# Attention and two MLPs on one core: high parts of probabilities on ScalarE, other costs and priorities in the scheduler

## The chip, the cores and the metric

One core of a Trainium2 chip, one launch. TensorE multiplies, VectorE, ScalarE and GpSimd do the elementwise work, SP (SyncE) issues every DMA of this kernel. The metric is the device time of the launch in microseconds (us); less is better.

## The reference

For 4 batches of 8 heads, 576 positions and head size 64: scores = q k^T / 8, a mask that lets a position see its own block of 64 and all earlier ones, softmax, product with v. The heads are laid side by side to x (2304 x 512). Two MLPs follow:

```
x = attention(q, k, v)                                   # 2304 x 512
h = x @ moe_w_in;  x = (max(h,0) + alpha*min(h,0)) @ moe_w_out     # 512 -> 2048 -> 512
h = x @ moe2_w_in; out = (h * sigmoid(1.702 h)) @ moe2_w_out
```

All inputs of attention are fp32; the four weight matrices and alpha arrive as 64-bit values (weights) and fp32, and the result is fp32.

## The kernel before

**Arithmetic.** A product of fp32 precision is made of three matmuls: each operand is split into a high part (a rounded copy, `hi_part`, ScalarE, L120) and a low part (the difference, `lo_part`, L123, on GpSimd or VectorE). So `gemm1` (L207) is 12 matmuls for one block of 128 hidden units, `g2_half` (L245 to 247) and `g2` (L653) likewise. Weights arrive as 64-bit words and are first narrowed on ScalarE and VectorE (`narrow`, L150 to 156), then split.

**Attention** runs in passes, a pass being a batch and a pair of heads. Queries are cut into five tiles `QT` (64 or 128 rows against 64, 192, 320, 448 or 576 keys); tiles 0 to 2 form one group, 3 and 4 another; a group is worked in two slots. The first batch takes its passes group by group (all four pairs for group one, then for group two), the others both groups in one pass. For a slot: `score` (TensorE, L441); `soft` (the minimum on VectorE, L456, the exponential with its sum on ScalarE, L464); when both slots of a group are through, `norm` (VectorE, L473 and 474) makes the factors. Then for each head `high` (L486) writes the factor times the exponentials as fp16, on GpSimd, one instruction per tile, and `rest` (VectorE, L494) writes the same product less that fp16 value, as a second fp16 part. A DMA transpose (L498, issued by SP) turns both parts, `pv` (L519) multiplies them with V, and `pv_out` (ScalarE L531, VectorE L532) adds up and sends x to DRAM. The exponentials have four buffers (`EB`), two per slot, so the exponentials of the next group wait for the rests of this one; scores have two PSUM buffers.

**MoE, first layer, first half** (hidden blocks 0 to 7) runs in eight blocks of 288 tokens as soon as attention has made them, in between the rest of attention: `gemm1`, `gate` (ScalarE L215, VectorE L216), `gate_split` (L120, L123), `g2_half`. It has two PSUM banks, shared with `warm` (L584), 174 filler matmuls on constants that are planned between the slots of the first batch. One bank belongs to the fillers until the last of them, planned behind the scores of the 14th slot, is through; gemm1 of the second hidden block needs that bank. After attention come the second half of the first layer and the whole second layer in blocks of 384 tokens (L207 and L653 in turn).

**What sets the order.** All work is first listed with a kind and a step. `arrange` then simulates the five engines: among the instructions of an engine whose inputs are there, it issues the one with the lowest place, which is the step plus a tenth of the kind's `ORDER` plus the kind's `SHIFT`. Times for that simulation come from `cost` and from the DMA terms in `arrange` (issue, transfer, landing). The order that results is fixed for each engine; on the chip every engine executes its list strictly in order and waits by semaphores. `HI_ACT` names the tiles whose high part goes to ScalarE; it is empty before.

Of the kernel before, what the change touches and what calls it, by code (L numbers as in the profile page):

```python
# [19 lines left out]
DRAM = bass.MemoryType.DRAM  # L20
# [25 lines left out]
    "split x 2": 8, "load w": 9, "load w 2": 9, "load x": 9, "load k": 9.5, "load q": 9.5, "load v": 9.5, "load alpha": 9.6,  # L46
}
SHIFT = {
    "gate": -44.2, "gate 2": -23, "gemm1": 56.7, "gemm1 2": 12.5, "gemm2": 12.8, "half": 58.9, "half out": -42,
    "high": -6.3, "load alpha": 27.7, "load k": 56.1, "load q": -37.1, "load v": -27.1, "load w": -32.6,  # L50
    "load w 2": -53.5, "load x": -33, "narrow": 56.5, "narrow 2": -25.1, "norm": -46.2, "out": -53.7,
    "prep out": 42.4, "prep t": 41.2, "prep v": 41.6, "pv": -10, "pv out": -41.9, "rest": 40.6, "score": 51.7,
    "setup": -24.2, "soft": 19, "split g": -43.8, "split g 2": 4.8, "split w": 7.8, "split w 2": -28.1,
    "split x": 26.4, "split x 2": 57.1, "warm": 56.9,
}
BIG = 1.0e30

# [2 lines left out]
def kernel(  # L60
# [65 lines left out]
    PTB = 2  # L126
    W = {}
    EB = 4
    HI_ACT = ()
    words = {}  # L130

    def load_w(u):
# [159 lines left out]
    def hl_part(j, x, m, n, h):  # L292
        o = 128 * (QT[j][4] + x * QT[j][3])
        return hl[0 if j < 3 else 1][h][0:m, o + 64 * h:o + 64 * h + n]
# [181 lines left out]
    def high(n, h):  # L476
        for y in (n - 1, n):
            stat, es, tiles = st[y, "e"]
            for a, j, off in tiles:
                q0, m, nk, ch, c0 = QT[j]  # L480
                r = stat[0:m, 2, 2 * a + h:2 * a + h + 1]
                o, e = hl_part(j, 0, m, nk, h), es[h][0:m, off:off + nk]
                if j in HI_ACT:
                    act.activation(out=o, in_=e, func=ACTF.Copy, scale=r)
# [51 lines left out]
    for u, (i, g, s) in enumerate(slots):  # L536
        n = 2 * u
# [12 lines left out]
    for i in range(len(passes)):  # L550
# [8 lines left out]
        for z, what in enumerate(todo):  # L559
            n = n0 + z * (cnt - (i == N0)) // len(todo)  # L560
# [110 lines left out]
    for z, (u, f) in enumerate(seq):  # L671
        n = n2 + z
# [5 lines left out]
    for y, u in enumerate(units):  # L678
        n = start[u]
# [10 lines left out]
    for n, order, z, fn, place in sorted(plan, key=lambda o: o[:3]):  # L690
        places.append((len(nc.cur_bb.bb.instructions), place, order == ORDER["warm"]))
        fn()
    arrange(tc, nc, places)


# [17 lines left out]
def free_size(ap):  # L713
    n = 1
    for _, c in list(ap.ap)[1:]:
        n *= c
    return n


def box(ap):  # L720

    t, size, dims = ap.tensor, BYTES[ap.dtype], list(ap.ap)
    if t.space == PSUM:
        return 0, 128, 0, 1 << 20
    pitch = t.shape[-1] if t.space == DRAM else dims[0][0]
    r0, c0 = divmod(ap.offset, pitch)
    r1 = r0 + 1 + sum((n - 1) * s // pitch for s, n in dims if s >= pitch)
    c1 = c0 + 1 + sum((n - 1) * s for s, n in dims if s < pitch)
    return r0, r1, c0 * size // 64 * 64, -(-c1 * size // 64) * 64


def dma_run(ap):

    n = 1
    for s, c in reversed(list(ap.ap)):
        if s != n:
            break
        n *= c
    return n * BYTES[ap.dtype]


def mode(w):

    rows, cols = list(w.ap)[0][1], free_size(w)
    return tuple(32 if n <= 32 else 64 if n <= 64 else 128 for n in (rows, 128 if BYTES[w.dtype] == 4 else cols))


def takes_port(eng, kind, ins, outs):

    if eng == "Pool":  # L750
        return True
    if eng != "DVE" or not ins or any(a.tensor.space == PSUM for a in ins + outs) or kind == "InstTensorReduce":
        return False
    n = max(free_size(a) for a in outs)
    return sum(free_size(a) == n for a in ins) > 1 or "TensorScalar" in kind or "TensorCopy" in kind


def cost(eng, kind, ins, outs):

    n = max(free_size(a) for a in ins + outs)  # L760
    psum = any(a.tensor.space == PSUM for a in ins)
    if eng == "PE":
        mv, w = ins[:2]
        cols, load = free_size(outs[0]) * (2 if mv.dtype == F32 else 1), free_size(w)
        rows = list(w.ap)[0][1]
        each = 13.3 if mv.dtype == F32R else 2.7
        return cols / 2.4 + each, load / 1.2 + 13.3 if BYTES[w.dtype] == 4 else load / 4.8, cols * rows / 128, mode(w)
    if eng == "Activation":
        return (50 if psum else 93) + n / 1.2 + (187 if len(outs) > 1 else 0),
    full = sum(free_size(a) == n for a in ins)  # L770
    if eng == "Pool":
        return (35 + n / 1.2 if not ins else 244 + n / 1.2 if full < 2 else 148 + 2.1 * n),
    if not ins:
        return (40 if outs[0].tensor.space == PSUM else 7) + n / 1.92,
    if psum and len(ins) < 3 or n < 8 or kind == "InstTensorReduce":
        return 65 + n / 0.96,
    if full < 2:
        return 64 + n / 1.92,
    return (129 if len(ins) > 2 else 68) + n / 0.96,


def arrange(tc, nc, places):
# [4 lines left out]
    for x, i in enumerate(nc.cur_bb.bb.instructions):  # L787
        ins, outs = ([a.bass_ap for a in z if getattr(a, "bass_ap", None) is not None] for z in (i.ins, i.outs))
        if type(i).__name__ in ("BassTilePoolBoundary", "InstRegisterMove") or not outs:
            continue  # L790
        while at + 1 < len(places) and places[at + 1][0] <= x:
            at += 1
        k, need = len(todo), set()
        for rw, ap in [(0, a) for a in ins] + [(1, a) for a in outs]:
            t = ap.tensor
            if t.name.startswith("in_"):
                continue
            tag = getattr(t, "tag", None)
            if tag and t.space != DRAM:
                ring = rings.setdefault(tag, [])  # L800
                if t.name not in users:
                    users[t.name] = set()
                    ring.append((t.tag_meta.bufs, users[t.name]))
                users[t.name].add(k)
            rw = rw or t.space == PSUM
            b = box(ap)
            w, r = writes.setdefault(t.name, []), reads.setdefault(t.name, [])
            for z in w + (r if rw else []):
                if z[4] != k and z[0] < b[1] and b[0] < z[1] and z[2] < b[3] and b[2] < z[3]:
                    need.add(z[4])  # L810
            if rw:
                for l in (w, r):
                    l[:] = [z for z in l if not (b[0] <= z[0] and z[1] <= b[1] and b[2] <= z[2] and z[3] <= b[3])]
            (w if rw else r).append((*b, k))
        eng = i.engine.name
        kind = type(i).__name__
        if eng == "PE":
            if places[at][2] and last_pe is not None:
                need.add(last_pe)
            last_pe = k  # L820
        if kind in ("InstDMACopy", "InstDmaTransposeAnt"):
            a = outs[0]
            size = free_size(a) * list(a.ap)[0][1] * BYTES[a.dtype]
            if kind == "InstDMACopy":

                run = min(dma_run(z) for z in ins + outs)
                t = size / run * (8.3 + 0.0368 * run) / 16
                inside = all(z.tensor.space != DRAM and not z.tensor.name.startswith("in_") for z in ins + outs)
                c = (580 if inside else 400 if run > 512 else 500, 2 * t if inside else t, 1000 if outs[0].tensor.space == DRAM or inside else 1600)
            else:  # L830
                c = (0.0046 * size - 100, size / 32768 * 130, 2400 - 0.0046 * size)
            ports.append(False)
        else:
            c = cost(eng, kind, ins, outs)
            ports.append(takes_port(eng, kind, ins, outs))
        todo.append((i, eng, kind, c, places[at][1]))
        preds.append(need)
# [47 lines left out]
    while coming or any(waiting.values()):  # L885
        while coming and coming[0][0] <= now:
            t, k = heappop(coming)
# [4 lines left out]
        for e in names:  # L892
            while waiting[e] and free[e] <= now:
                k = heappop(waiting[e])[1]
                orders[e].append(todo[k][0])
                _, _, kind, c, _ = todo[k]
                if e == "SP":
                    t = now
                    free[e] = t + c[0] + 70
                    end = ring_end = max(t + c[0] + c[2], ring_end) + c[1]  # L900
                elif e == "PE":

                    slow = seen[int(now / TICK) - 1] < 3060
                    t = now + max(0, c[1] * (1 + slow) - pe_last - (now - pe_end))
                    if c[3] != pe_mode:
                        t, pe_mode = max(t, pe_end + DRAIN), c[3]
                    pe_last = (c[0] - 2.7) * 2 if slow else c[0]
                    end = free[e] = pe_end = t + pe_last
                    while t < end:
                        z = min(end, (int(t / TICK) + 1) * TICK + 0.01)  # L910
                        seen[int(t / TICK)] += c[2] * (z - t) / pe_last
                        t = z
# [41 lines left out]
```

## Time and profile before

| | us |
|---|---|
| median of 3 runs | 1084.31 (1083.62 to 1084.81) |
| the profiled execution | 1087.33, span 1085.5 |
| TensorE busy | 1021.4 (94%) |
| VectorE busy | 604.3 (56%) |
| ScalarE busy | 494.7 (46%) |
| GpSimd busy | 462.4 (43%) |

Busy shares are averages over stages with different limits: attention and the first half of the first layer end near 470 us, and TensorE has little idle time after 190 us. PE is TensorE, PEld its weight load, DVE VectorE, ACT ScalarE, POOL GpSimd, and SPq the queue of SyncE. A releaser ("<-ACT e L464") is what ended a wait.

### The profile page before, as it was taken

How to read it: one execution, taken by the hardware profiler on the slowest of the kernel's cores; microseconds unless marked ns; L12 is line 12 of the kernel's file. 1: busy time of each engine (PE TensorE's matmuls, PEld its weight loads, DVE VectorE, ACT ScalarE, POOL GpSimd, SP SyncE). 2: the span in 40 equal slices, each digit the busy share in tenths (PEclk: the TensorE clock that was granted, in tenths of full speed). 3: DMA queues.
4: the chain of work that ended last, by engine and by line, in shares of the span. 5: the costliest groups of instructions: out<-in, count | busy, mean ns of one | idle time of the engine just before them, and what ended most of it. 6: DMA issues, size and time to landing. Idle time of an engine off the chain costs nothing. (4 is left out here: it accounts for less than half of the span.)

```text
span 1085.5 us, 17180 instructions
## 1 busy us (share of the span) xinstructions
PE 1021.4 (94%) x6454; PEld 934.3 (86%) x6454; DVE 604.3 (56%) x1029; ACT 494.7 (46%) x1164; POOL 462.4 (43%) x494
## 2 busy tenths in 40 slices
PE   7776978999999999999999999999999999999998
PEld 4554867989898899999999999899999999999997
DVE  7888998788888885778883236831111121211110
ACT  5664765666566564565543235433223232322322
POOL 4565864656666574644432233422222222222221
PEclk8888999999999999999999999999999999999999
DMA  7897989788989765544643225401000010000000
GB/s 190 189 209 156 209 188 187 138 176 155 175 154 175 147 124 140 168 141 157 202 144 126 81 65 183 146 8 59 1 30 30 1 59 1 30 30 1 30 1 30
DMA packets 257284, 120.28 MB, mean 111 GB/s; under 512 B 213936, under 2 KB 250800, under 8 KB 257200
## 3 DMA queue, kind: packets, MB, share of 16 engines
q1 hardware_dynamic: 257200, 119.18, 46.1%
q8 instruction: 51, 0.84, 0.3%
q14 instruction: 33, 0.27, 0.1%
HBM read 68.82 MB, written 18.87 MB: 81 GB/s over the span
## 5 line engine op out<-in xcount | busy, mean ns | idle before, releaser
L123 POOL TENSOR_TENSOR gs<-g,gs 128x384 fp32r<-128x384 f32 (+1 forms) x208 | 212.8, 1024 | 452.4 <-ACT gs L120 431.8
L207 PE MATMUL h<-xh,wh 128*128 128x384 f32 (+1 forms) x832 | 272.2, 327 | 6.8 <-ACT xo L251 3.7
L207 PE MATMUL h<-xh,wl 128*128 128x384 f32 (+1 forms) x832 | 270.2, 325 | 0.0
L219 DVE TENSOR_TENSOR g<-g,h 128x384 f32<-128x384 f32 x96 | 53.1, 553 | 291.6 <-ACT g L218 291.6
L653 PE MATMUL acc<-wh,gs 128*128 128x512 f32 x576 | 194.9, 392 | 1.5 <-DVE o L663 1.5
L207 PE MATMUL h<-xl,wh 128*128 128x384 f32 x576 | 193.1, 335 | 0.0
L207 PEld LDWEIGHTS h<-xh,wh 128*128 128x128 f32 x832 | 156.3, 188 | 15.3 <-ACT xo L251 5.2
L207 PEld LDWEIGHTS h<-xh,wl 128*128 128x128 f32 x832 | 156.4, 188 | 0.1
L120 ACT ACTIVATE gs<-g 128x384 fp32r<-128x384 f32 (+1 forms) x208 | 103.3, 498 | 106.7 <-DVE g L219 60.9
L218 ACT ACTIVATE g<-h 128x384 f32<-128x384 f32 x96 | 47.0, 490 | 191.6 <-PE h L207 191.6
L486 POOL TENSOR_SCALAR hl<-e,stat 64x64 f16<-64x64 f32 (+4 forms) x160 | 107.7, 688 | 57.1 <-DVE stat L474 28.0
L653 PEld LDWEIGHTS acc<-wh,gs 128*128 128x128 f32 x576 | 108.1, 188 | 22.4 <-DVE o L663 1.3
L494 DVE SCALAR_TENSOR_TENSOR hl<-e,stat,hl 64x64 f16<-64x64 f32 (+4 forms) x160 | 122.7, 800 | 5.7 <-POOL hl L486 4.7
L653 PE MATMUL acc<-wl,gs 128*128 128x512 f32 x288 | 113.7, 395 | 0.0
L207 PEld LDWEIGHTS h<-xl,wh 128*128 128x128 f32 x576 | 108.1, 188 | 4.1
L519 PE MATMUL pv<-pt,vp 128*128 128x256 f16 (+2 forms) x960 | 88.1, 248 | 14.6 <-DMA pt<-hl 10.5
L464 ACT ACTIVATE e<-sc,stat 64x64 f32<-64x64 f32 (+4 forms) x160 | 82.8, 520 | 34.0 <-DVE hl L494 19.2
L653 PE MATMUL acc<-gs,wh 128*128 128x384 f32 x384 | 98.1, 335 | 0.2 <-DVE o L663 0.2
L216 DVE SCALAR_TENSOR_TENSOR g<-g,nalph,h 128x288 f32<-128x288 f32 (+1 forms) x112 | 61.6, 551 | 58.4 <-ACT g L215 57.4
L519 PEld LDWEIGHTS <-vp 128*128 128x128 bf16 x960 | 64.6, 102 | 27.6 <-DMA pt<-hl 14.9
L123 POOL TENSOR_TENSOR wl<-sq,wh 128x512 fp32r<-128x512 f32 x40 | 59.5, 1488 | 61.7 <-ACT wh L120 61.6
L245 PE MATMUL x<-gs,wh 128*128 128x288 f32 x256 | 75.7, 302 | 2.9 <-ACT wh L120 2.4
(65 smaller groups left out, 1708.4 us busy)
## 6 DMA issues: line engine op xcount, KB each, us to landing
rw<-in_moe_w_in_dram SPq DMA_DIRECT2D x32, 512.0 KB, 4.2
rw<-in_moe_w_out_dram SPq DMA_DIRECT2D x32, 512.0 KB, 3.8
nat_q<-in_q_dram SPq DMA_DIRECT2D x24, 288.0 KB, 4.1
nat_k<-in_k_dram SPq DMA_DIRECT2D x16, 288.0 KB, 3.6
nat_v<-in_v_dram SPq DMA_DIRECT2D x16, 288.0 KB, 4.5
xa<-xo SPq DMA_DIRECT2D x32, 144.0 KB, 2.5
o<-xa SPq DMA_DIRECT2D x24, 192.0 KB, 2.5
xl<-xs SPq DMA_DIRECT2D x6, 768.0 KB, 4.9
```

Source lines behind the costliest of these rows:

```text
L120: act.activation(out=dst, in_=src, func=ACTF.Copy, scale=scale_)
L123: eng.tensor_tensor(out=dst, in0=src, in1=hi.bitcast(F32), op=ALU.subtract)
L207: pe.matmul(ps, st_[:, sl], mv[:, c], start=z == 0, stop=z == 3 * KD - 1)
L216: dve.scalar_tensor_tensor(out=g, in0=g, scalar=nalph[:, f:f + 1], in1=ps, op0=ALU.mult, op1=ALU.add)
L218: act.activation(out=g, in_=ps, func=ACTF.Sigmoid, scale=1.702)
L219: dve.tensor_tensor(out=g, in0=g, in1=ps, op=ALU.mult)
L245: pe.matmul(ps, oh[:, sl], gh, start=f == 0, stop=False)
L464: act.activation(out=eo, in_=v[:, h] if len(heads) > 1 else v, func=ACTF.Exp, scale=-1.0, bias=stat[0:m, 0, a:a + 1], accum_out=stat[0:m, ...
L486: pool.tensor_scalar(out=o, in0=e, scalar1=r, scalar2=1.0, op0=ALU.mult, op1=ALU.mult)
L494: dve.scalar_tensor_tensor(out=hl_part(j, 1, m, nk, h), in0=es[h][0:m, off:off + nk], scalar=stat[0:m, 2, 2 * a + h:2 * a + h + 1], in1=hl ...
L519: pe.matmul(o, l, r, start=z == 0, stop=z == len(ops) - 1)
L653: pe.matmul(ps, a, b_, start=f == f0 and z == 0, stop=f == NF - 1 and z == 2)
```

## The change

The set of tiles in `HI_ACT` goes from none to all five. In `high` the branch for ScalarE is then taken for every tile, so all 160 high parts are activations with the factor as a per-row scale:

```
if j in HI_ACT:
    act.activation(out=o, in_=e, func=ACTF.Copy, scale=r)
else:
    pool.tensor_scalar(out=o, in0=e, scalar1=r, scalar2=1.0, op0=ALU.mult, op1=ALU.mult)
```

In the scheduler's simulation, VectorE's reads of PSUM and reductions of 8 or more columns count 155 ns instead of 65 beside the time per column, and DMA landings count 250 ns (plain) or 600 ns (transposes) later. `SHIFT` gets a new value for nearly every kind.

```diff
--- before.py
+++ after.py
@@ -46,12 +46,12 @@
     "split x 2": 8, "load w": 9, "load w 2": 9, "load x": 9, "load k": 9.5, "load q": 9.5, "load v": 9.5, "load alpha": 9.6,
 }
 SHIFT = {
-    "gate": -44.2, "gate 2": -23, "gemm1": 56.7, "gemm1 2": 12.5, "gemm2": 12.8, "half": 58.9, "half out": -42,
-    "high": -6.3, "load alpha": 27.7, "load k": 56.1, "load q": -37.1, "load v": -27.1, "load w": -32.6,
-    "load w 2": -53.5, "load x": -33, "narrow": 56.5, "narrow 2": -25.1, "norm": -46.2, "out": -53.7,
-    "prep out": 42.4, "prep t": 41.2, "prep v": 41.6, "pv": -10, "pv out": -41.9, "rest": 40.6, "score": 51.7,
-    "setup": -24.2, "soft": 19, "split g": -43.8, "split g 2": 4.8, "split w": 7.8, "split w 2": -28.1,
-    "split x": 26.4, "split x 2": 57.1, "warm": 56.9,
+    "gate": -5.6, "gate 2": 3.5, "gemm1": 58, "gemm1 2": 12.5, "gemm2": 12.5, "half": 55.1, "half out": -40.2,
+    "high": 14.8, "load alpha": 30.8, "load k": 48.3, "load q": -16.4, "load v": -13.4, "load w": 42,
+    "load w 2": -8.5, "load x": 21.6, "narrow": 49, "narrow 2": 21.5, "norm": -15, "out": -55.1,
+    "prep out": 29.6, "prep t": 14.3, "prep v": 33.9, "pv": 8.2, "pv out": -26.5, "rest": 11.7, "score": 53.6,
+    "setup": -59.4, "soft": 5.6, "split g": -25.7, "split g 2": 33.6, "split w": 22.7, "split w 2": 22.6,
+    "split x": 28.2, "split x 2": -47.3, "warm": 59.1,
 }
 BIG = 1.0e30
 
@@ -126,7 +126,7 @@
     PTB = 2
     W = {}
     EB = 4
-    HI_ACT = ()
+    HI_ACT = (0, 1, 2, 3, 4)
     words = {}
 
     def load_w(u):
@@ -773,7 +773,7 @@
     if not ins:
         return (40 if outs[0].tensor.space == PSUM else 7) + n / 1.92,
     if psum and len(ins) < 3 or n < 8 or kind == "InstTensorReduce":
-        return 65 + n / 0.96,
+        return (65 if n < 8 else 155) + n / 0.96,
     if full < 2:
         return 64 + n / 1.92,
     return (129 if len(ins) > 2 else 68) + n / 0.96,
@@ -826,9 +826,9 @@
                 run = min(dma_run(z) for z in ins + outs)
                 t = size / run * (8.3 + 0.0368 * run) / 16
                 inside = all(z.tensor.space != DRAM and not z.tensor.name.startswith("in_") for z in ins + outs)
-                c = (580 if inside else 400 if run > 512 else 500, 2 * t if inside else t, 1000 if outs[0].tensor.space == DRAM or inside else 1600)
+                c = (580 if inside else 400 if run > 512 else 500, 2 * t if inside else t, 1250 if outs[0].tensor.space == DRAM or inside else 1850)
             else:
-                c = (0.0046 * size - 100, size / 32768 * 130, 2400 - 0.0046 * size)
+                c = (0.0046 * size - 100, size / 32768 * 130, 3000 - 0.0046 * size)
             ports.append(False)
         else:
             c = cost(eng, kind, ins, outs)
```

## Rows read from the trace of the kernel before

**Rows 1.** Table by stage: window, length, busy us of PE, PEld, DVE, ACT, POOL.
```profile
0.00:109.00 109.00, 78.39 (x495) 54.01 (x495) 88.90 (x166) 61.09 (x157) 59.94 (x77) 0.86 0.84 186
109.00:190.00 81.00, 66.40 (x524) 58.57 (x523) 73.38 (x134) 50.53 (x137) 52.53 (x57) 0.97 0.95 194
190.00:300.00 110.00, 105.85 (x908) 99.48 (x905) 90.61 (x184) 70.83 (x203) 68.79 (x86) 0.99 0.84 159
300.00:400.00 100.00, 95.45 (x817) 89.40 (x815) 86.43 (x170) 63.00 (x189) 62.35 (x78) 1.00 0.80 153
400.00:450.00 50.00, 48.36 (x385) 46.75 (x383) 31.23 (x47) 24.76 (x60) 26.88 (x26) 1.00 0.57 154
```

**Rows 2.** The chain that ended last, in order of time: start, us, what.
```profile
691.16 2.10 PE h L207 x12
```

**Rows 3.** Fillers (L584) by stage: PE, PEld; timeline of PE near 112 us.
```profile
0.00:109.00 109.00, 39.82 (x169) 17.89 (x169) 0.86 0.84 186
...
111.98 0.98 PE L584 MATMUL warm<-mk_l 128*128 128x384 bf16 x5
112.66 0.43 PE L207 MATMUL h<-xh,wh 128*128 128x288 f32 x1
```

**Rows 4.** Timeline of DVE, norm lines (L473) of the first and eighth group.
```profile
23.01 0.83 DVE L473 TENSOR_SCALAR stat<-stat 128x6 f32<-128x6 f32 x1 [0.28 <-ACT e L464]
...
122.46 0.74 DVE L473 TENSOR_SCALAR stat<-stat 128x4 f32<-128x4 f32 x1
```

**Rows 5.** Groups by shape: rests (L494), a high part (L486); busy, mean ns.
```profile
L494 DVE SCALAR_TENSOR_TENSOR hl<-e,stat,hl 128x576 f16<-128x576 f32 x32 | 35.8, 1118 | 0.2
L494 DVE SCALAR_TENSOR_TENSOR hl<-e,stat,hl 128x448 f16<-128x448 f32 x32 | 33.0, 1030 | 1.6 <-POOL hl L486 1.1
...
L486 POOL TENSOR_SCALAR hl<-e,stat 128x576 f16<-128x576 f32 x32 | 29.7, 928 | 0.0
...
L494 DVE SCALAR_TENSOR_TENSOR hl<-e,stat,hl 128x320 f16<-128x320 f32 x32 | 22.3, 697 | 0.8 <-POOL hl L486 0.7
...
L494 DVE SCALAR_TENSOR_TENSOR hl<-e,stat,hl 64x64 f16<-64x64 f32 x32 | 20.9, 655 | 2.7 <-POOL hl L486 2.7
...
L494 DVE SCALAR_TENSOR_TENSOR hl<-e,stat,hl 128x192 f16<-128x192 f32 x32 | 16.0, 501 | 0.4 <-POOL hl L486 0.2
```

**Rows 6.** Rests (L494, DVE), then high parts (L486, POOL) by stage.
```profile
0.00:109.00 109.00, 23.55 (x32) 0.86 0.84 186
109.00:190.00 81.00, 22.16 (x28) 0.97 0.95 194
...
0.00:109.00 109.00, 19.87 (x32) 0.86 0.84 186
109.00:190.00 81.00, 22.36 (x30) 0.97 0.95 194
```

**Rows 7.** Timeline: a rest under high parts, then rests alone.
```profile
215.10 2.05 POOL L486 TENSOR_SCALAR hl<-e,stat 64x64 f16<-64x64 f32 x5 [2.85 <-DVE stat L474]
...
215.45 0.95 DVE L494 SCALAR_TENSOR_TENSOR hl<-e,stat,hl 64x64 f16<-64x64 f32 x1 [0.45 <-POOL hl L486]
...
68.04 0.26 DVE L494 SCALAR_TENSOR_TENSOR hl<-e,stat,hl 64x64 f16<-64x64 f32 x1
...
369.10 1.42 DVE L494 SCALAR_TENSOR_TENSOR hl<-e,stat,hl 128x448 f16<-128x448 f32 x2
```

**Rows 8.** Groups by line and shape: ScalarE copies from SBUF to SBUF.
```profile
L120 ACT ACTIVATE gs<-g 128x288 fp32r<-128x288 f32 x64 | 28.0, 441 | 14.3 <-DVE g L216 14.0
...
L395 ACT ACTIVATE vp<-nat_v 128x576 bf16<-128x576 f32 x32 | 21.7, 679 | 0.6 <-POOL nat_v L396 0.3
```

**Rows 9.** Minimum over 576 columns (L456); PE waits from 0 to 190 us.
```profile
L456 DVE TENSOR_REDUCE stat<-sc 128x1 f32<-128x576 f32 x32 | 23.9, 748 | 0.4
...
PE pv L519 <- DMA pt<-hl: 8.0, 4, 4.0
PE tp L345 <- DMA nat_k<-in_k_dram: 5.1, 3, 2.6
```

## The prediction

> **What bounds the kernel now.** I read the table by stage first. After 190 us TensorE is the bound: it is busy for 95 to 97% of the stretches from 190 to 450 us [rows 1], and the chain that ended last, read next, is matmuls upon matmuls from 691 us on; the row shown is one of its pieces, a gemm1 of 12 matmuls in 2.10 us [rows 2]. The time that TensorE loses lies ahead of that. From 0 to 109 us it is busy for 78.4 us, but 39.8 of these are fillers, the warm matmuls [rows 1, 3]; so 109 - 38.6 = 70 us are lost there. From 109 to 190 us it idles 14.6 us, from 190 to 450 us another 4.2 + 4.5 + 1.6 = 10.3 us [rows 1]. The work of TensorE is fixed, so the kernel gets shorter by what is saved of these, above all of the 70.
>
> What holds the first stage? The MoE matmuls cannot start in earnest before the last fillers are through: five of them run at 111.98 us, and the row right behind is the first full gemm1 at 112.66 us [rows 3]. The fillers are tied in program order to the scores of the first 14 slots, so that moment is set by the pace of attention. The pace is read from the norm line: 23.01 us for the first group, 122.46 us for the eighth, seven periods of 14.2 us [rows 4]. In the first two stages VectorE is the fullest of the elementwise engines: 88.9 of 109 us (82%), then 73.4 of 81 (91%), against ScalarE's 61.1 and 50.5 and GpSimd's 59.9 and 52.5 [rows 1]. A group's chain also runs through it three times (minimum, norm, rest). I take VectorE as the bound of the early pace.
>
> **The change, part by part. What VectorE gets back.** GpSimd loses 160 high parts, 32 of each of five shapes, 62 of them before 190 us [rows 6]. The rest instruction (L494) reads two tiles and runs beside the next tile's high part. Beside GpSimd it is slow: the 64x64 form took 0.95 us from 215.45, inside a run of five high parts that began at 215.10 and lasted 2.05; alone it took 0.26 us, and the forms of 448 and 576 columns together 1.42 us alone [rows 7]. The straight line through these (0.20 us + 1.0 ns per column) gives 0.39 and 0.52 us at 192 and 320 columns, and a mean of (0.26 + 0.39 + 0.52 + 1.42)/5 = 0.52. The means of the run are 0.655, 0.501, 0.697, 1.030 and 1.118 us [rows 5]. Up to 109 us, 32 rests took 23.6 us where 32 x 0.52 = 16.6 would do: 7.0 us too much. From 109 to 190 us 28 took 22.2 against 14.6: 7.6 too much [rows 6]. Bounds: all of it goes (only high parts were in the way), or only their share of GpSimd's time, 19.9 of 59.9 = one third [rows 1, 6], since the splits of weights, gates and V stay on GpSimd. Rests run next to high parts by construction, so I take two thirds: 4.7 and 5.1 us.
>
> The Trainium skill's page SBUF — State Buffer, section Who interferes with whom, explains the 0.95 us and says more: a VectorE instruction with two SBUF inputs and a GpSimd one that reads SBUF take turns on a shared port, the loser blocks for the whole instruction, and ScalarE is never part of it. By this rule a stall behind a high part goes entirely, but an overlap with GpSimd's remaining work still blocks as before, so the rule allows both my bounds; the first rival is its full form.
>
> **What ScalarE gets.** The same 160 as activations. Copies from SBUF to SBUF took 679 ns at 576 columns and 441 at 288 [rows 8], 0.83 ns per column, so 572, 466, 360 and 254 ns at 448, 320, 192 and 64: mean 0.466 us, 160 x 0.466 = 75 us in all. That is 32 x 0.466 = 14.9 us in the first stage and 30 x 0.466 = 14.0 in the second, and brings ScalarE to 76.0 of 109 and 64.5 of 81 us, 70 and 80% of the present lengths [rows 1, 6]. No loading of another function table comes with it, since copies already stand between the exponentials on this engine. I cost it at nothing on the path, covered by the spare 20 to 30%. Without that cover high parts queue behind exponentials and gates behind high parts; the second rival prices this. What the chain gains: the first high part of a group comes out sooner, 0.62 us (19.87/32) before, 0.47 after [rows 6], and at 576 columns 0.68 in place of 0.93 [rows 5, 8]: 0.2 us per group, 1.4 us in seven.
>
> **What it comes to.** Up to 112 us: VectorE 4.7 us shorter and the chain 1.4, 0.9 us per period. VectorE is the fullest engine there, and I take all of it: -6 us. From 109 to 190 us VectorE gains 5.1 us, but TensorE already has MoE work there and idles 14.6 of 81 us: I take half, -2.5 us. From 190 to 450 us TensorE idles 10.3 us in all: a little comes from VectorE, a little is lost to ScalarE, 0.
>
> **The scheduler's table.** It times nothing on the chip; it only alters the order. A VectorE read of PSUM now counts 155 ns + columns/0.96, 755 ns at 576 columns, where the trace has 748; with 65 it was 665 [rows 9]. Landings are taken as later, so consumers are placed later in TensorE's queue. That can remove TensorE's waits for landings up to 190 us, of which the two largest are 8.0 us for transposed probabilities and 5.1 us for K [rows 9]; from the other side an order that fits worse can double them. Bounds -13 to +13 us. Before 112 us only fillers would take the place of a wait, which gains nothing, so I take -1.5 us, a share of the later ones.
>
> **The priorities.** On TensorE the order of the kinds stays: products with V, transposes, scores, then MoE and fillers. On VectorE it stays norm, gate, soft, rest, preparation, narrowing. On ScalarE high parts come behind exponentials and ahead of the splits of weights. On SP the loads of weights fall from ahead of the Q loads to far behind them; they share that one queue with the transposes, which wait in it for the rests, and what stands behind such a wait comes later by it. The first weights are needed for the full gemm1 at 112.66 us [rows 3] only, so a load late by a period of 14 us is hidden, except the last ones of the 16 before it. No price: 0, within the bounds of the table.
>
> Sum: -6 - 2.5 - 1.5 = -10 us. The profiled execution took 1087.33 us with a span of 1085.5, 3 us above the median 1084.31; the difference is applied to the median: **1074 us**.
>
> **Rivals.** (1) Much more: all contention with high parts goes, and the whole burst of a group comes out sooner. Up to 112 us 7.0 us of VectorE plus seven times 5 x (0.62 - 0.47) = 5.3 us, from 109 to 190 us 7.6 us, and half of the later 10.3, 5.2: -25 us, 1059 us. For it: 0.95 against 0.26 us. Against: 40 us of other GpSimd work remain before 109 us.
> (2) ScalarE becomes the bound: slower. Place: 109 to 450 us, where gemm1 has two PSUM banks, which the gate's Relu (L215) on ScalarE helps to free. 160 - 32 = 128 high parts run there, in 128/5 = 26 groups; a group puts 5 x 0.466 = 2.3 us on ScalarE in a burst. The other bank covers one gemm1: 2.10 us at 384 columns [rows 2], 1.6 at the 288 of these blocks. If each burst stands ahead of a gate, 26 x 0.7 = 18 us are lost, less the 8.5 gained: +9.5, 1094 us. It decides once gates regularly wait for over 1.6 us. For it: ScalarE at 80% from 109 to 190 us. Against: the gates stand ahead of high parts in the new priorities (-5.6 against 14.8).
> (3) The early pace is held by landings and hand-overs, not by VectorE's load, which leaves 20 of 109 us idle [rows 1]. Then only the later part of the sum stays in some measure, -2 us: 1082 us. Against: no engine idles for less in the stage.
>
> **How the numbers follow.** Forecast (1067 to 1080 us) 0.52; rival (1) 0.20; (2) 0.16; (3) 0.12. A measurement of this kernel tells a change from none at about 0.2%, 2.2 us. Faster: 0.52 + 0.20 + a third of (3) = 0.76; within 0.2%: the rest of (3), 0.08; slower: 0.16. The range that leaves out 2 in 10 runs from 1059, the middle of rival (1), to 1089, within rival (2).
>
> **What would show it.** Right: rests at a mean near 0.6 us, norms about 13.3 us apart, the first full gemm1 near 106 us, fewer fillers' time, VectorE's busy time up to 450 us down by 25 us or more, ScalarE's up by 65 to 75. Wrong: rests still at 0.8 us (other GpSimd work was in the way), the period unchanged (rival 3), or TensorE waiting for ScalarE's L215 and L464 for over 10 us between 109 and 450 us (rival 2).

## The result and the profile after

The changed kernel takes 1066.57 us (median of 4 runs, 1065.31 to 1069.64), before 1083.96 (4 runs): a ratio of 0.9842 with an interval of 0.9821 to 0.9863, 1.6% faster. The forecast was 1074 us: it had 10 us gained, and 17 were. The profiled execution took 1065.89 us, span 1064.0, so 21.5 us less span than before.

The table by stage of the changed kernel, to be read against [rows 1] (window, its length, busy us of PE, PEld, DVE, ACT, POOL, with the count of instructions; then PE's granted clock, DMA share, GB/s):

```profile
0.00:109.00 109.00, 80.54 (x535) 55.14 (x536) 94.64 (x176) 78.62 (x197) 44.04 (x46) 0.92 0.92 199
109.00:190.00 81.00, 73.99 (x612) 68.06 (x610) 69.22 (x145) 69.86 (x190) 33.76 (x33) 1.00 0.90 191
190.00:300.00 110.00, 103.72 (x874) 96.27 (x873) 86.51 (x191) 91.89 (x258) 33.10 (x35) 0.97 0.90 167
300.00:400.00 100.00, 98.76 (x858) 93.64 (x857) 72.52 (x160) 79.37 (x222) 32.92 (x33) 1.00 0.80 159
400.00:450.00 50.00, 48.74 (x370) 48.09 (x369) 35.76 (x49) 29.13 (x63) 27.90 (x24) 1.00 0.46 145
```

The count of PE's matmuls, in brackets behind its busy time, tells more than the busy shares, since 6454 matmuls are run in either kernel. By 109 us 535 have started against 495, by 190 us 1145 against 1017 (a matmul that runs across the end of a stage is counted in both rows of the table, so these are a little less than the sums of its rows). When does the changed kernel reach the count that the other has at a given time? It starts its 495th matmul at 103.1 us, its 1017th at 173.7, its 1922nd (before at 300 us) at 288.0 and its 3118th (before at 450 us) at 431.9. So it leads by 6, 16, 12 and 18 us at 109, 190, 300 and 450 us, and by 21.5 us at the end: three quarters of the final lead stand by 190 us, though a part is lost again by 300 us. TensorE's busy time fell too, by 7 us for the same matmuls:

```profile
PE 1014.2 (95%) x6454; PEld 931.0 (87%) x6454; DVE 576.4 (54%) x1029; ACT 561.5 (53%) x1324; POOL 363.6 (34%) x334
```

The granted clock fits that: 0.92 and 1.00 of 2.4 GHz in the first two stages against 0.86 and 0.97 [rows 1], so less of that time was granted at 1.2 GHz. From 190 to 300 us it is a little lower than before, 0.97 against 0.99.

Rests and high parts by shape after (columns as in [rows 5]; mean ns is the number before the second bar):

```profile
L494 DVE SCALAR_TENSOR_TENSOR hl<-e,stat,hl 128x576 f16<-128x576 f32 x32 | 28.8, 900 | 0.3 <-ACT hl L484 0.3
L484 ACT ACTIVATE hl<-e,stat 128x576 f16<-128x576 f32 x32 | 24.5, 765 | 0.0
...
L494 DVE SCALAR_TENSOR_TENSOR hl<-e,stat,hl 128x448 f16<-128x448 f32 x32 | 22.8, 712 | 1.2 <-ACT hl L484 1.0
...
L494 DVE SCALAR_TENSOR_TENSOR hl<-e,stat,hl 128x320 f16<-128x320 f32 x32 | 19.1, 596 | 0.4
...
L494 DVE SCALAR_TENSOR_TENSOR hl<-e,stat,hl 128x192 f16<-128x192 f32 x32 | 13.6, 424 | 0.8 <-ACT hl L484 0.3
...
L484 ACT ACTIVATE hl<-e,stat 64x64 f16<-64x64 f32 x32 | 10.9, 340 | 4.9 <-DVE stat L474 1.9 <-ACT qs L120 1.5 <-issue 1.4
...
L494 DVE SCALAR_TENSOR_TENSOR hl<-e,stat,hl 64x64 f16<-64x64 f32 x32 | 10.3, 323 | 2.5 <-ACT hl L484 2.3
```

The 64x64 rest went from 655 to 323 ns, the mean of all from 0.80 to 0.59 us: the rests are nearly as fast as alone (0.26 and 1.42 us in [rows 7]). VectorE's busy time up to the end fell by 27.9 us (604.3 to 576.4).

The trace also tells which rests are slow. In the changed kernel 124 of the 160 rests have no GpSimd instruction beside them and take 0.51 us in the mean; the other 36 take 0.87 us. Before, only 28 had none beside them. By shape such a rest takes the same in both kernels: 0.27, 0.40 or 0.41, 0.53 or 0.54, 0.68 or 0.66, and 0.81 or 0.80 us. Taken over these lengths, the 160 rests lost 42.0 us before and lose 8.5 us after.

The norms, first, seventh, eighth and last group, and the last fillers with the first full gemm1 (timelines, answering to [rows 4] and [rows 3]):

```profile
21.02 0.17 DVE L473 TENSOR_SCALAR stat<-stat 128x6 f32<-128x6 f32 x1 [0.38 <-ACT e L464]
...
100.75 0.16 DVE L473 TENSOR_SCALAR stat<-stat 128x4 f32<-128x4 f32 x1
...
119.23 0.16 DVE L473 TENSOR_SCALAR stat<-stat 128x4 f32<-128x4 f32 x1
...
385.74 0.17 DVE L473 TENSOR_SCALAR stat<-stat 128x4 f32<-128x4 f32 x1 [0.76 <-ACT e L464]
```

```profile
104.76 0.98 PE L584 MATMUL warm<-mk_l 128*128 128x384 bf16 x5
105.44 0.43 PE L207 MATMUL h<-xh,wh 128*128 128x288 f32 x1
```

Before, the seventh and the last norm were these:

```profile
107.96 0.17 DVE L473 TENSOR_SCALAR stat<-stat 128x4 f32<-128x4 f32 x1
...
406.50 0.17 DVE L473 TENSOR_SCALAR stat<-stat 128x4 f32<-128x4 f32 x1 [0.23 <-ACT e L464]
```

Six periods up to the seventh norm take 13.3 us each, before 14.2. The eighth follows late, at 119.23 us, so that seven periods take 14.0 us each, before 14.2. The full gemm1 has TensorE from 105 us on, just ahead of that late norm; whether it is what delays it was not tried. From the eighth to the last, 24 periods take 11.1 us each, before 11.8: attention ends 21 us sooner.

TensorE's two waits for landings up to 190 us, answering to [rows 9]:

```profile
PE pv L519 <- DMA pt<-hl: 3.8, 3, 1.6
...
PE tp L345 <- DMA nat_k<-in_k_dram: 1.9, 1, 1.9
```

A third one grew, the wait for Q; before and then after:

```profile
PE tp L345 <- DMA nat_q<-in_q_dram: 3.5, 2, 2.5
```

```profile
PE tp L345 <- DMA nat_q<-in_q_dram: 6.2, 5, 2.5
```

The three together fell from 16.6 to 11.9 us.

### The profile page after: what moved, and what is told of

It is laid out like the page before. It is cut to its first block, busy times and chain, and to the rows that moved or that the text cites. A ratio compares the mean times of both kernels' runs of the same rounds, so it can differ in the third digit from the quotient of the medians.

```text
span 1064.0 us, 17161 instructions
## 1 busy us (share of the span) xinstructions
PE 1014.2 (95%) x6454; PEld 931.0 (87%) x6454; DVE 576.4 (54%) x1029; ACT 561.5 (53%) x1324; POOL 363.6 (34%) x334
## 4 chain that ended last, share of the span: by engine, by line
PE 64%; DMA 1%; DVE 1%; ACT 1%; issue 0%; ACTq 0%; DVEq 0%
PE h L207 31%; PE acc L653 28%; PE x L245 1%; PE x L246 1%; PE x L247 1%; PE pv L519 1%; DMA xa<-xo 1%; PE sc L441 0%; DMA out_dram<-o 0%; DVE hl L494 0%; DVE g L216 0%; ACT hl L484 0%; ACT o L666 0%; DVE wl L123 0%; DVE wa L153 0%
## 5 line engine op out<-in xcount | busy, mean ns | idle before, releaser
L123 POOL TENSOR_TENSOR gs<-g,gs 128x384 fp32r<-128x384 f32 (+1 forms) x208 | 222.8, 1072 | 483.8 <-ACT gs L120 475.5
L519 PE MATMUL pv<-pt,vp 128*128 128x256 f16 (+2 forms) x960 | 84.5, 242 | 8.9 <-DMA pt<-hl 7.6
L215 ACT ACTIVATE g<-h 128x288 f32<-128x288 f32 (+1 forms) x112 | 49.0, 440 | 83.2 <-PE h L207 75.5
L494 DVE SCALAR_TENSOR_TENSOR hl<-e,stat,hl 64x64 f16<-64x64 f32 (+4 forms) x160 | 89.5, 591 | 5.1 <-ACT hl L484 3.8
L464 ACT ACTIVATE e<-sc,stat 64x64 f32<-64x64 f32 (+4 forms) x160 | 82.4, 517 | 5.6 <-DVE stat L456 5.1
L484 ACT ACTIVATE hl<-e,stat 64x64 f16<-64x64 f32 (+4 forms) x160 | 78.2, 551 | 9.8 <-DVE stat L474 4.6
## 6 DMA issues: line engine op xcount, KB each, us to landing
nat_q<-in_q_dram SPq DMA_DIRECT2D x24, 288.0 KB, 4.1
nat_k<-in_k_dram SPq DMA_DIRECT2D x16, 288.0 KB, 3.3
nat_v<-in_v_dram SPq DMA_DIRECT2D x16, 288.0 KB, 3.8
```

What stands on the lines that cost most here:

```text
L123: eng.tensor_tensor(out=dst, in0=src, in1=hi.bitcast(F32), op=ALU.subtract)
L215: act.activation(out=g, in_=ps, func=ACTF.Relu, scale=-1.0)
L464: act.activation(out=eo, in_=v[:, h] if len(heads) > 1 else v, func=ACTF.Exp, scale=-1.0, bias=stat[0:m, 0, a:a + 1], accum_out=stat[0:m, ...
L494: dve.scalar_tensor_tensor(out=hl_part(j, 1, m, nk, h), in0=es[h][0:m, off:off + nk], scalar=stat[0:m, 2, 2 * a + h:2 * a + h + 1], in1=hl ...
L519: pe.matmul(o, l, r, start=z == 0, stop=z == len(ops) - 1)
```

## The experiments

Times are medians; "before" ran beside each group at 1084.5 us (first four), 1085.9 (next four) and 1083.8 (last four). "Started" is the count of matmuls by 450 us.

| run | high parts on | order | us | ratio to before (95%) | started |
|---|---|---|---|---|---|
| before | GpSimd | its own | 1084.0 | 1 | 3118 |
| after | ScalarE | its own | 1066.6 | 0.9842 (0.9821 to 0.9863) | 3241 |
| e1 | ScalarE | of before | 1087.3 | 1.0027 (1.0007 to 1.0047) | 3115 |
| e2 | GpSimd | of after | 1092.3 | 1.0068 (1.0043 to 1.0093) | 3062 |
| e3 | ScalarE, and dummy reads on GpSimd | of after | 1081.3 | 0.9960 (0.9940 to 0.9980) | 3122 |
| e4 | GpSimd | new table, new priorities | 1097.8 | 1.0114 (1.0082 to 1.0146) | 3025 |
| e5 | ScalarE | old table, old priorities | 1092.7 | 1.0056 (1.0037 to 1.0075) | 3122 |
| e6 | ScalarE | old table, new priorities | 1086.2 | 0.9997 (0.9984 to 1.0009) | 3124 |
| e7 | ScalarE | new table, old priorities | 1080.0 | 0.9937 (0.9915 to 0.9958) | 3143 |
| e8 | ScalarE | new both, fewer fillers | 1085.4 | 0.9987 (0.9969 to 1.0005) | 3078 |
| e9, e10 | GpSimd | before, priorities jittered | 1097.4, 1086.8 | 1.0120 (1.0093 to 1.0147), 1.0020 (1.0000 to 1.0040) | 3057, 3114 |
| e11, e12 | ScalarE | after, priorities jittered | 1075.5, 1072.0 | 0.9913 (0.9888 to 0.9938), 0.9877 (0.9852 to 0.9903) | 3177, 3195 |

**The engine and the order, crossed (e1, e2).** A kernel's order can be kept while the high parts change their engine: the simulation goes on believing that they run where they ran, and each engine's list is sorted out afterwards by the real engine. Every other engine then has its list unchanged, instruction for instruction.

```diff
-        eng = i.engine.name
+        eng = "Pool" if i.engine.name == "Activation" and "hl" in outs[0].tensor.name else i.engine.name
...
-    orders = {e: [] for e in names}
+    orders = defaultdict(list)
...
-                orders[e].append(todo[k][0])
+                orders[todo[k][0].engine.name].append(todo[k][0])
```

(e1, with `HI_ACT` full in the kernel before; e2 is the mirror image, with `HI_ACT` empty in the changed one and the two engines exchanged.)

> The order of every engine is the one of before; only the 160 high parts run on ScalarE, at the places in time where the plan of before had them on GpSimd. Theory 1 (rests and high parts contend, VectorE sets the early pace): rests near 0.6 us, VectorE's busy time about 30 us less, time 1070 to 1078 us. Rival (the new order made the gain, the engine did not): 1082 us or more, and up to 1092 if high parts stand ahead of gates on ScalarE.

> The order of every engine is the one of after; only the 160 high parts run on GpSimd, at the places in time where the plan of after had them on ScalarE. Theory 1: rests back to about 0.75 to 0.8 us, time back to 1078 to 1088 us. Rival (the order made the gain): 1064 to 1070 us, rests may be slow all the same.

e1 is as theory 1 has it in the rests, and in the rival's range in time. The rests did get fast, and VectorE was relieved (574.6 us busy against 604.3); the time got no shorter (1087.3 us). Its groups of rests and high parts on the page:

```profile
L494 DVE SCALAR_TENSOR_TENSOR hl<-e,stat,hl 64x64 f16<-64x64 f32 (+4 forms) x160 | 93.0, 606 | 12.0 <-ACT hl L484 10.3
...
L484 ACT ACTIVATE hl<-e,stat 64x64 f16<-64x64 f32 (+4 forms) x160 | 83.1, 552 | 14.3 <-DVE stat L474 12.7 <-ACT e L464 1.0 <-ACT qs L120 0.2
```

What took the place is in ScalarE's queue. In its timeline the four high parts of one group (norm at 151.34 us), in e1 and then in after (norm at 146.73 us):

```profile
151.93 0.67 ACT L484 ACTIVATE hl<-e,stat 128x448 f16<-128x448 f32 x1 [1.45 <-DVE stat L474]
152.50 0.63 ACT L120 ACTIVATE wh<-sq 128x512 fp32r<-128x512 f32 x1
153.04 0.76 ACT L484 ACTIVATE hl<-e,stat 128x576 f16<-128x576 f32 x1
...
154.77 0.66 ACT L484 ACTIVATE hl<-e,stat 128x448 f16<-128x448 f32 x1
...
157.03 0.76 ACT L484 ACTIVATE hl<-e,stat 128x576 f16<-128x576 f32 x1
```

```profile
148.34 2.56 ACT L484 ACTIVATE hl<-e,stat 128x448 f16<-128x448 f32 x4 [1.26 <-DVE stat L474]
```

After runs the four in one piece of 2.56 us. In e1 they lie between other work that stood in ScalarE's list anyway (copies of weights, keys and queries, an output of pv, an exponential; not all of it is shown), and take 5.9 us from the first start to the last end (157.79 less 151.93). Their rests wait for that: the page gives 12.0 us of VectorE idle ahead of rests in e1, 5.1 in after. Later exponentials are late too. TensorE's waits of that kind from 109 to 450 us (us in total, times, longest), in before, in e1 and then in after:

```profile
PE sc L441 <- ACT e L464: 5.2, 9, 1.3
```

```profile
PE sc L441 <- ACT e L464: 11.3, 13, 3.4
```

```profile
PE sc L441 <- ACT e L464: 2.4, 7, 0.8
```

The last norm of e1 stands at 407.17 us, where before had it at 406.50. By the count of matmuls e1 leads before by 2 us at 109 and at 190 us, and by nothing from 400 us on. So VectorE's relief did not shorten attention as a whole in an order made for a ScalarE with 75 us less to do; late high parts and late exponentials are what the trace shows in its place, and whether they are the whole of it was not tried. e2 is as theory 1 has it in the rests (0.79 us) but slower than forecast (1092.3 us against 1078 to 1088), and it refutes the rival that the order made the gain: the order of after costs 26 us more when the high parts stay on GpSimd.

**GpSimd's share by itself (e3).** After in its own order, and one more read of GpSimd beside each rest, counted as free by the simulation so that no other list changes:

```diff
-                    act.activation(out=o, in_=e, func=ACTF.Copy, scale=r)
+                    act.activation(out=o, in_=e, func=ACTF.Copy, scale=r); pool.tensor_scalar(out=spare[0:m, 0:min(nk, 448)], in0=o[:, 0:min(nk, 448)], scalar1=r, scalar2=1.0, op0=ALU.mult, op1=ALU.mult)
```

> After, in its own order, with one more GpSimd instruction per high part, which reads the finished high part and writes a scratch tile (448 columns at most), as long as a high part on GpSimd and beside the rest; nobody waits for it but GpSimd's own later work. Theory 1: the rests slow down from 0.56 to 0.7 us or more, VectorE's busy time up to 450 us rises by 20 us or more, time rises by 5 to 12 us. Rival (it is ScalarE's shorter high part and its place in the chain that gain): rests may slow, the time stays within 3 us of after.

```profile
L484 POOL TENSOR_SCALAR spare<-hl,stat 128x448 f16<-128x448 f16 (+3 forms) x160 | 125.3, 783 | 66.7 <-ACT hl L484 55.5 <-POOL spare L484 0.2
...
L494 DVE SCALAR_TENSOR_TENSOR hl<-e,stat,hl 64x64 f16<-64x64 f32 (+4 forms) x160 | 97.9, 645 | 4.5 <-ACT hl L484 3.2
```

The time came back by 14.7 us (1081.3 against 1066.6), more than expected, while the rests slowed by less, from 0.59 to 0.65 us in place of 0.7 or more. So 125 us of GpSimd work beside the rests undo most of the gain, but the rests account for 8 us of VectorE only. VectorE's other work did not slow down as a whole: VectorE's busy time over the whole execution rose by 5.5 us (576.4 to 581.9), less than the rests' share, where 20 us or more up to 450 us were expected. What did grow are waits for GpSimd's later work, which now stands behind the dummies. ScalarE's wait for it up to 450 us, in after and then in e3:

```profile
ACT vp L395 <- POOL nat_v L396: 2.5, 6, 1.1
```

```profile
ACT vp L395 <- POOL nat_v L396: 10.4, 10, 2.3
```

So e3 is not a clean price of the contention: a part of its 14.7 us is GpSimd's queue. How much is which stays open.

**Which part of the order (e4 to e7).** Table and priorities exchanged by the values of the diff, planned anew each time.

> The new table and the new priorities, planned anew with the high parts on GpSimd. Theory 1: the planner knows of the shared port and can only spread the loss: 1078 to 1086 us. Rival (table and priorities made the gain): 1064 to 1072 us.

> High parts on ScalarE, old table, old priorities; the planner makes a new order that knows of the move. Run e1 had the move in the old order and gained nothing. Theory A (any order that knows where the high parts run will do): 1066 to 1074 us. Theory B (the new priorities or the table are needed, since the old ones put high parts ahead of exponentials on ScalarE): 1078 to 1090 us.

> Move and new priorities, old table. Theory A: 1066 to 1072 us, like e5. Theory B with the priorities as the cause: 1065 to 1070 us while e5 stays above 1078. With the table as the cause: 1075 us or more.

> Move and new table, old priorities. Theory A: 1066 to 1072 us. Theory B with the priorities as the cause: within 5 us of e5, above 1076. With the table as the cause: 1065 to 1070 us.

e4 refutes the rival that table and priorities alone gain: without the move they lose 1.1%, 12 us more than theory 1 allowed. e5 refutes theory A: a planner that knows of the move does not find the gain with the old table and priorities (1092.7 us). e6 and e7 are each faster than e5, by 6 and 13 us, but only both together reach 1066.6. e6 lies where the table was to be the cause (1075 us or more), e7 in none of the ranges given for it. Whether the table or the priorities weigh more these four do not settle, as the next group shows: one planned order differs from a neighbouring one by as much.

**How much is luck of one order (e9 to e12).** Each of the 35 priorities moved by a random amount of at most 1 (a slot is 2 steps), the same amounts for before and after. Of e11, the first lines:

```diff
-    "gate": -5.6, "gate 2": 3.5, "gemm1": 58, "gemm1 2": 12.5, "gemm2": 12.5, "half": 55.1, "half out": -40.2,
+    "gate": -6.3, "gate 2": 4.2, "gemm1": 58.5, "gemm1 2": 12.0, "gemm2": 12.5, "half": 55.0, "half out": -39.9,
...
```

> Before, with each of its 35 priorities moved by a random amount of at most 1 (a slot is 2 steps), planned anew. Selection theory (either set of priorities gives one picked order, whose neighbours are worse): 1090 to 1100 us. Rival (the order is robust): within 5 us of 1084.

> As e9 with other random amounts. Selection theory: 1090 to 1100 us. Rival: within 5 us of 1084.

> After, with the same amounts as e9. Selection theory: 1076 to 1088 us, some 10 us under e9, which would be the worth of the move itself between orders that nobody picked. Rival (robust order): within 5 us of 1066.

> After, with the same amounts as e10. Selection theory: 1076 to 1088 us, some 10 us under e10. Rival: within 5 us of 1066.

Before's neighbours are 13.4 and 2.8 us slower than it, after's 8.9 and 5.4: all four neighbours are slower than the order that they were made from, so either kernel stands on a picked order. How much that is worth is less clear: only e9 lies in the selection theory's range, e10 lies in the rival's (within 5 us of 1084), e11 half a microsecond below the selection theory's, and e12 between the two. The pairs with equal jitter differ by 21.9 and 14.8 us, the kernels themselves by 17.4. So in the two pairs tried the gain of the whole change does not hang on one lucky order, though it was expected at 10 us here.

**Does the first full gemm1 set the end (e8)?** `W3` from 28 to 22, so 30 fillers fewer:

> After, with fillers only up to the scores of the 11th slot (W3 from 28 to 22), planned anew; 30 fillers fewer. If the last filler holds the full gemm1 back: first full gemm1 at 84 to 95 us in place of 105, time 1055 to 1063 us. Rival (inputs, weights or VectorE hold it, the fillers only cover the wait): full gemm1 still after 100 us, time within 4 us of after, or longer by a lower granted clock.

The full gemm1 did come early (the last five fillers, then its matmuls):

```profile
83.97 0.99 PE L584 MATMUL warm<-mk_l 128*128 128x384 bf16 x5
84.66 0.43 PE L207 MATMUL h<-xlb,wh 128*128 128x288 f32 x1
```

but the time is 18.8 us longer than after. The table by stage shows where: from 109 to 300 us TensorE idles more (15.9 and 14.3 us, in after 7.0 and 6.3), at a lower granted clock (0.92 and 0.94):

```profile
0.00:109.00 109.00, 86.37 (x583) 63.34 (x584) 93.01 (x175) 79.75 (x206) 48.36 (x53) 0.91 0.90 193
109.00:190.00 81.00, 65.15 (x493) 57.59 (x492) 64.40 (x127) 61.84 (x161) 27.72 (x26) 0.92 0.90 187
190.00:300.00 110.00, 95.74 (x778) 86.26 (x777) 81.65 (x181) 84.14 (x233) 26.92 (x27) 0.94 0.83 157
```

By 109 us e8 has started 439 of the kernel's own matmuls against 361 in after (583 and 535, less 144 and 174 fillers), but by 300 us 1706 against 1844. The early start moves MoE work forward and not attention, whose last norm comes 20 us later than in after (385.74):

```profile
405.42 0.17 DVE L473 TENSOR_SCALAR stat<-stat 128x4 f32<-128x4 f32 x1 [0.18 <-ACT e L464]
```

So an early first gemm1 is not enough. Why attention got slower was not tried, and since e8 is planned anew, a part of its 18.8 us may be the scatter between orders, up to 13 us above. Nor is the end of attention the whole of the time: e5 has its last norm only 3.6 us later than after, and takes 26 us longer.

```profile
389.34 0.17 DVE L473 TENSOR_SCALAR stat<-stat 128x4 f32<-128x4 f32 x1 [1.70 <-ACT e L464]
```

## Why the prediction was right, point by point

- **Direction, time, range: right, with luck in the sum.** 1066.6 us lies in 1059 to 1089, just on the fast side of the likeliest case's own range (1067 to 1080). But the sum had VectorE's relief and the shorter chain gain 8.5 us by themselves, with ScalarE's load and the priorities at nothing. By itself the move costs 3 us (e1); the gain came from the move and the order together.
- **Contention of rests with high parts: right, and shown.** Rests at 0.59 us (near 0.6 was forecast) in after, 0.61 in e1, but 0.79 in e2 and 0.80 before: it follows the engine, whatever the order. Four fifths of what the rests lost beside GpSimd are gone (42.0 to 8.5 us), where two thirds were assumed. The shared port as the Trainium skill's page SBUF — State Buffer tells it, section Who interferes with whom, agrees with this: the rests keep a part of their stalls beside GpSimd's other work (0.32 us at 64 columns against 0.26 alone).
- **First stage, -6 us: right in size, not by its cause alone.** The lead at 109 us is 6 us, the full gemm1 comes at 105.44 us (near 106 forecast), the period to the seventh norm is 13.3 us (13.3 forecast), though to the eighth, as the forecast had measured it, it is 14.0. But e1, where VectorE's rests are as much relieved in this stage (18.7 us for 32, 23.6 before), leads before by 2 us only: relief of VectorE was not the whole of what held the early pace. And e8 speaks against one thing said beside it, that the moment of the first full gemm1 sets the end.
- **109 to 190 us, -2.5 us: mis-sized.** The lead grows by 10 us there. TensorE idles 7.0 us in place of 14.6, and its clock is granted in full. VectorE gained more than the 5.1 us assumed: 30 rests took 15.3 us where 28 had taken 22.2, 7.9 us less for as many. "Half, since TensorE already has MoE work there" failed, with the order of after: as much as VectorE gained, and more, went through. In e1 the lead does not grow at all there. Later stages added 5 us where 0 was forecast.
- **Two signs that did not come.** VectorE's busy time up to 450 us fell by 12 us (370.5 to 358.6), not by 25 or more; by then the changed kernel has done more of VectorE's other work, and over the whole execution it is 27.9. The fillers took 39.7 us in place of 40.8, hardly less.
- **ScalarE at nothing on the path: right only with the new order.** This is the step that was missing from the sum. In the order of before the move alone costs 3 us (e1), with the high parts scattered in ScalarE's queue and exponentials late: a milder relative of rival (2), which had gates late instead. With the order of after ScalarE is at 86% from 109 to 190 us (69.86 of 81) and TensorE waits 2.4 us for its exponentials from 109 to 450 us, where e1 waits 11.3.
- **Priorities at 0: wrong.** With the high parts on ScalarE, the order of after is worth 20.7 us against that of before (1087.3 to 1066.6); with them on GpSimd it costs 8. The sum added the parts up, but move and order are one thing: -17 together, +3 and +8 apart. One reading was wrong beside it: at the same step the weight loads did not stand ahead of the Q loads before (-32.6 against -37.1, and the lowest place goes first); no price hung on it.
- **Table, -1.5 us: not settled.** The two waits for landings fell from 13.1 to 5.7 us up to 190 us, in the range given, but the wait for Q rose by 2.7 us. e7 against e5 would say -13 us and after against e6 -20, both more than the term; but one order differs from the next by 3 to 13 us, so two such pairs do not give its size.
- **ScalarE's unit cost: too low.** 0.551 us a high part, not 0.466; its busy time up to 450 us rose by 78.7 us (270.2 to 348.9), where 65 to 75 was forecast.
- **Rivals.** (3), a pace held by landings and hand-overs, is not refuted: the period to the seventh norm fell to 13.3 us where the order changed too, but in e1, with VectorE relieved in the old order, it is 13.9 (14.2 before). What holds it there was not tried. (2) is refuted for the changed kernel: TensorE waits 2.4 us for L464 from 109 to 450 us, and none for L215 is listed. Its sign, over 10 us, is seen in e1 (11.3), but by exponentials and not by gates, at a cost of 3 us and not 9.5. (1) had the better size, 25 us, but not its place: it put half in the first stage, which gave 6.

## What to carry to other kernels

When work moves to another engine in a kernel with fixed in-order queues, price the move and the order as one: here the relief of one engine turned into time only once the order was made for it. Before crediting a re-planned kernel's gain to one of its edits, keep the order and exchange the engine, and jitter the planner's inputs to see how far neighbouring orders differ; here that was up to 13 us, as much as most of the effects in question. An early start of filling work may gain nothing if what feeds it does not get faster: the one run that tried it lost 18.8 us.

## What the runs showed of the hardware that was not expected

- A ScalarE activation with a per-row scale read from SBUF took 765 ns at 576 columns and 340 at 64, 86 ns more than the line through plain copies gives (679 at 576, 254 at 64 by the line of [rows 8]), with the same slope of 0.83 ns per column. Input and output types of the copies differ in part from those of the high parts; which of the differences costs it was not measured.
- Which of the two starts first decides whether a rest is slowed. In the traces of before, after, e1, e2 and e3 all 800 rests were looked at: the 357 that began while GpSimd was not running anything (a GpSimd instruction may have begun under them) took no more than 0.02 us over the length that their shape has alone. The slow ones all began while a GpSimd instruction was already running: 117 in before, 0.36 us longer in the mean, and 24 in after, 0.36 us longer too.
- So an extra GpSimd instruction beside each rest slowed the rests far less than the high parts had (0.65 against 0.80 us), though it took no less time (0.78 against 0.69 us in the mean, its own waits included; it reads fp16, the high part fp32): it is released by the same high part as the rest, and where the rest begins first, GpSimd's instruction is the one that is stretched. In e3 a rest of 64 columns took its usual 0.28 us; the dummy of 64 columns that began 0.07 us after it, and ran on beside later rests, took 3.30 us, where the shortest took 0.31:

```profile
142.45 0.28 DVE L494 SCALAR_TENSOR_TENSOR hl<-e,stat,hl 64x64 f16<-64x64 f32 x1
142.52 3.30 POOL L484 TENSOR_SCALAR spare<-hl,stat 64x64 f16<-64x64 f16 x1 [1.45 <-ACT hl L484]
```
